# Row-maximum spread matmuls moved back in TensorE's order, and v's maxima taken one tile ahead

## The chip, the cores and the metric

The kernel runs on one core of a Trainium2 chip. The metric is the device time of one execution in microseconds (us). Five engines run beside each other, each taking its own instructions in order: TensorE (PE, the matmuls; PEld is its weight load), VectorE (DVE), ScalarE (ACT), GpSimd (POOL) and SyncE (SP, which here issues the transfers). They wait for each other through semaphores.

## The reference

Three parts follow one another on a batch of 4, 12 heads, 448 positions and 64 elements a head (768 in all):

```python
def _attn_ref(q, k, v):
    scores = scale * np.matmul(q, k.transpose(0, 1, 3, 2)) - np.log(S)
    attn = 1.0 / (1.0 + np.exp(-scores))
    return np.matmul(attn, v).astype(np.float32)

def _moe_ref(x, w_ch1, w_ch2):
    X = np.fft.fft(x, axis=1)
    X = np.fft.fft(X, axis=2)
    u = x + np.real(X)
    mu = np.mean(u, axis=-1, keepdims=True)
    var = np.mean((u - mu) ** 2, axis=-1, keepdims=True)
    un = (u - mu) / np.sqrt(var + 1e-06)
    ch = np.maximum(un @ w_ch1, 0.0) @ w_ch2
    return (u + ch).astype(np.float32)

def _moe2_ref(x, w_val, conv_w, w_out):
    for k in range(K):
        gate_pre += conv_w[k][None, None, :] * xp[:, k:k + S, :]
    gate = 1.0 / (1.0 + np.exp(-gate_pre))
    val = x @ w_val
    return (gate * val @ w_out).astype(np.float32)
```

## The kernel before

**Number formats.** The large products are made of f16 halves: a tensor is scaled by a power of two, rounded to f16 (`hi`, `hh`, `ph`, `xs` and so on), and what is left over is a second f16 tensor (`lo`, `hl`, `pl`). Each product takes three matmuls. The power of two comes from the largest absolute value of the tensor: v for each batch (it scales the Fourier mixing), w1 and w2 of the first weight group, and x2, the FFN's output, for each batch.

**The maximum and its spread.** `amax` (L104) reduces a tile to a column of row maxima. When all columns are there, `peak_row` (L107) reduces them to one column `t` and multiplies the identity `eye` by it, which gives the diagonal tile `pd` (L112, VectorE; one buffer). `peak_spread` (L115, the matmul at L118, TensorE) multiplies a matrix of ones by `pd`, so that each row of a PSUM tile holds all 128 maxima. `peak_max` (L121, the reduction at L123, VectorE) takes their maximum, and a chain of small operations makes the scale of it. The spread's tile is one of four `ps_m` buffers, which attention's output, the Fourier products, the norms, the down tiles and the value tiles share too. `peak` (L126) does the three as a generator: `wait` yields ahead of the spread, and as many behind it. Weights of later groups use `peak_pool`, which has no matmul.

**The order.** It is written by hand. The attention loop goes over 96 tiles, `t`, of two half heads; `b = t // 24` is the batch and `r = t % 24` the tile in it. In a tile TensorE gets the scores of tile t+1 (L356, L358) and, LAG tiles behind, the values (L381, L383); ScalarE the sigmoid (L369). `load_v` issues a v tile, `amax_v` takes its maximum, for four tiles at a time. `peak_v(b, k)` is step k of the three for v, and `scale_v` makes the scales. Three queues of generators are stepped within the loop: `fq` (Fourier mixing of the batch before), `lq` (norm) and `wq` (the conversion of 64-bit weights, `to_f32` and `split_weight`, on VectorE and ScalarE); `aq` is ScalarE's. VectorE's share in the loop is therefore the sum of maxima, folds (L399), weight conversion (L182 to L198), Fourier work (`eo`, `pl`, `zl`, L491, L494) and norm (L565 to L617).

**After the loop** the FFN runs as blocks of `up` (L730, ps_s) and `down` (L753, ps_m), weight group by weight group. Each yield of a block calls `background`, which steps the same queues; in the last group two steps of `wq` a call. ScalarE makes `hh` (L737), VectorE `hl` (L739) and adds down's product to `acc` (L757). As soon as `down` of the last group has finished batch b, `prep_x2(b)` is queued: six maxima (`xm`), the peak of them, the scale `sx`, then `xs` (ScalarE L795, VectorE L797). In the same stretch `first_gates` puts 24 convolution steps (L820) on VectorE. Then follow `value` (L907) and `project` (L932).

The steps of `peak` and the place of v's steps in the loop of the kernel before, in a few lines:

```python
    def peak(m, nm, wait):
        d = peak_row(m, nm)
        for _ in range(wait):
            yield
        p = peak_spread(d)
        for _ in range(wait):
            yield
        return peak_max(p, nm)
```

Of the kernel before, what the change touches and what calls it, by code (L numbers as in the profile page):

```python
# [17 lines left out]
B, H, S, D, DM, DFF = 4, 12, 448, 64, 768, 3072  # L18
CK = 112
NT = 6  # L20
# [41 lines left out]
def body(tc, qd, kd, vd, w1d, w2d, cwd, wvd, wod, cdd, k12d, csd, eyed, out):  # L62
# [60 lines left out]
        V.tensor_reduce(out=g, in_=p[:, :128], axis=AX.X, op=ALU.max)  # L123
        return g

    def peak(m, nm, wait):  # L126

        d = peak_row(m, nm)
        for _ in range(wait):
            yield  # L130
        p = peak_spread(d)
        for _ in range(wait):
            yield
        return peak_max(p, nm)

# [67 lines left out]
    def split_weight(pl, scratch, src, res, shape, exp, nm, bufs=1):  # L203

        n = shape[1] * shape[2]
        t = wp.tile([128, n], F32, tag="wf", bufs=1, name="wf")
        m = keep.tile([128, 18], F32, tag="wm", bufs=2, name="wm")
        step = scratch.cols
        yield from to_f32(scratch, src, t, n, m)
        yield  # L210
        m = m[:, :n // (step if step == WCOLS else step // 2)]
        g = yield from (peak(m, nm, 2) if step == WCOLS else peak_pool(m, nm))
        e, i = pow2(g, nm, True)
        s = scaled(i, 2.0 ** exp, nm + "s")
        yield
        scratch.idle = True
        while isinstance(pl, Later) and pl.at is None:
            yield
        scratch.idle = False
        step = scratch.cols  # L220
        hi = pl.tile(shape, F16, tag=nm + "hi", bufs=bufs, name=nm + "hi")
        lo = pl.tile(shape, F16, tag=nm + "lo", bufs=bufs, name=nm + "lo")
        res += [hi, lo, e]
        h, l = (x.rearrange("p a b -> p (a b)") for x in (hi, lo))
        for c in range(0, n, n // 4):
            cc = slice(c, c + n // 4)
            if step > WCOLS:
                A.activation(out=t[:, cc], in_=t[:, cc], func=AF.Copy, scale=s)
                A.activation(out=h[:, cc], in_=t[:, cc], func=AF.Copy)
                yield  # L230
                P.tensor_tensor(out=l[:, cc], in0=t[:, cc], in1=h[:, cc], op=ALU.subtract)  # L231
            else:
                yield from act(out=h[:, cc], in_=t[:, cc], func=AF.Copy, scale=s)
                V.scalar_tensor_tensor(out=l[:, cc], in0=t[:, cc], scalar=s, in1=h[:, cc], op0=ALU.mult, op1=ALU.subtract)
            yield
# [403 lines left out]
    for t in range(NHALF):  # L639
        i, g = t // 2, t % 2  # L640
        b = i // H
        r = t - b * 2 * H
        if t + 1 < NHALF:
            scores(t + 1)
        sigmoid(t)
        if t % 4 < 2 and t // 4 + 1 < NPAIR:
            (prep_k if t % 4 else prep_q)(t // 4 + 1)
        if t % 4 == 1 and t // 4 + 4 < NPAIR:
            load_qk(t // 4 + 4)
        if t % 4 == 1 and t // 4 + 2 < NPAIR:  # L650
            load_v(*divmod(t // 4 + 2, NT))
        if t % 4 == 2:
            amax_v(b, r // 4)
        if r == 23:
            peak_v(b, 0)
        if b and r == 0:
            peak_v(b - 1, 1)
        if b and r == 1:
            peak_v(b - 1, 2)
            scale_v(b - 1)  # L660
        if b and r == 2:
            fq.append(fourier(b - 1))
        step(fq)
        for n in range(3):
            if mixed.get(n) == 1:
                lq.append(norm(n))
            if n in mixed:
                mixed[n] += 1
        step(lq)
        if b == 0 and r in (6, 7, 8, 9):  # L670
            c, o = divmod(r - 6, 2)
            nc.sync.dma_start(out=cd[:, c, o], in_=cdd[:, c, o])
        if b == 0 and r == 12:
            nc.sync.dma_start(out=k12, in_=k12d)
        if b == 0 and r in (5, 6, 10, 11):
            c, o = divmod((5, 6, 10, 11).index(r), 2)
            cst.append(fk.tile([128, 3, 4 * NE], F32, tag="pm", bufs=2, name="cst")[:, :, :NP])
            nc.sync.dma_start(out=cst[-1], in_=csd[:, c, o])
        if b == 0 and r in (8, 9, 14, 15):
            c, o = divmod((8, 9, 14, 15).index(r), 2)  # L680
            push(out=cs[:, c, o], in_=cst.pop(0), func=AF.Copy)
        for n in range(2):
            if r == FOLD_AT + LAG + 4 * n:
                fold_part(b, n)
        if t > 6:
            credit[0] += W_RATE[0] if b == 0 else W_RATE[1] if r < 6 else W_RATE[2]
            step(wq, int(credit[0]))
            credit[0] %= 1
        drain(2 if t % 4 == 3 else 1)
        if t >= LAG:  # L690
            values(t - LAG)
            store_x(t - LAG)
    for t in range(NHALF - LAG, NHALF):
        values(t)
        store_x(t)
    peak_v(B - 1, 1)
    drain()
    finish(wq)
    peak_v(B - 1, 2)
    scale_v(B - 1)  # L700
    attn.close()


# [77 lines left out]
    def prep_x2(b):  # L781
        xs = acc[b][:, :, PAD:]
        m = keep.tile([128, NT], F32, tag="xm", bufs=2, name="xm")
        for j in range(NT):
            amax(xs[:, j], m, j)
            if j % 2:
                yield
        g = yield from peak(m, "x2", 1)
        e, i = pow2(g, "x2")
        sx = scaled(i, 2.0 ** X2_EXP, "sx")  # L790
        xs2 = homes[b].tile([128, NT, 2 * S], F16, tag=f"un{b}", name="xs")
# [249 lines left out]
```

## Time and profile before

| | us |
|---|---|
| time, median of 3 runs | 1113.61 (1111.94 to 1113.67) |
| the profiled execution | 1113.55 |
| its span, first to last instruction | 1111.8 |
| mean granted TensorE clock | 0.986 |
| TensorE busy | 1066.1 (96% of the span) |
| VectorE busy | 756.1 (68%) |
| ScalarE busy | 427.7 (38%) |
| GpSimd busy | 191.1 (17%) |

The span begins and ends with the first and the last instruction; the time of an execution holds a little more on both sides. Busy shares are means over stages that have different limits, so the rows below are read stage by stage. In a row of a timeline the first two numbers are start and duration in us, a group `x2` is two of the same form one behind the other, and the bracket at the end is the time that the engine stood idle ahead of it and what ended that. The granted clock is the share of full speed that TensorE was given.

### The profile page before, as it was taken

How to read it: one execution, taken by the hardware profiler on the slowest of the kernel's cores; microseconds unless marked ns; L12 is line 12 of the kernel's file. 1: busy time of each engine (PE TensorE's matmuls, PEld its weight loads, DVE VectorE, ACT ScalarE, POOL GpSimd, SP SyncE). 2: the span in 40 equal slices, each digit the busy share in tenths (PEclk: the TensorE clock that was granted, in tenths of full speed). 3: DMA queues.
4: the chain of work that ended last, by engine and by line, in shares of the span. 5: the costliest groups of instructions: out<-in, count | busy, mean ns of one | idle time of the engine just before them, and what ended most of it. 6: DMA issues, size and time to landing. Idle time of an engine off the chain costs nothing.

```text
span 1111.8 us, 15303 instructions
## 1 busy us (share of the span) xinstructions
PE 1066.1 (96%) x5616; PEld 550.7 (50%) x5616; DVE 756.1 (68%) x2154; ACT 427.7 (38%) x654; POOL 191.1 (17%) x171
## 2 busy tenths in 40 slices
PE   8899998989899999999999999999999967999998
PEld 4345453546455555555555555555555533555554
DVE  2866999697884676657676765676765679775530
ACT  5675656633232233333423233333233322343321
POOL 3322323331311111111101111110111100000000
PEclk9999999999999999999999999999999978999999
DMA  6723433011111322222333321233321100000001
GB/s 212 211 79 92 122 98 86 10 44 44 30 43 43 86 72 69 73 63 68 85 86 86 81 67 39 72 85 86 87 73 40 32 1 0 1 34 34 34 34 67
DMA packets 34780, 74.13 MB, mean 67 GB/s; under 512 B 3940, under 2 KB 11920, under 8 KB 34704
## 3 DMA queue, kind: packets, MB, share of 16 engines
q1 hardware_dynamic: 34704, 73.15, 23.2%
q8 instruction: 44, 0.72, 0.3%
q14 instruction: 32, 0.26, 0.1%
HBM read 67.46 MB, written 5.51 MB: 66 GB/s over the span
## 4 chain that ended last, share of the span: by engine, by line
PE 76%; DVE 16%; DMA 3%; ACT 3%; issue 1%; POOL 1%; SPq 0%; ACTq 0%; DVEq 0%; POOLq 0%
PE ps_s L730 26%; PE ps_m L753 26%; PE ps_m L932 7%; PE ps_m L907 7%; DMA w<-w1d 3%; PE ps_m L466 2%; PE ps_m L381 2%; PE ps_s L356 2%; PE ps_m L483 1%; DVE gp L820 1%; DVE wf L195 1%; DVE wf L198 1%; DVE xm L105 1%; DVE acc L757 1%; DVE wabs L190 1%
## 5 line engine op out<-in xcount | busy, mean ns | idle before, releaser
L730 PE MATMUL ps_s<-un,w1hi 128*128 128x448 f16 x1152 | 316.6, 357 | 3.5 <-DVE hl L739 3.5
L753 PE MATMUL ps_m<-hh,w2hi 128*128 128x448 f16 x576 | 205.1, 356 | 1.3 <-DVE acc L757 1.2
L730 PE MATMUL ps_s<-un,w1lo 128*128 128x448 f16 x576 | 205.5, 357 | 0.0
L753 PE MATMUL ps_m<-hl,w2hi 128*128 128x448 f16 x576 | 204.9, 356 | 0.0
L753 PE MATMUL ps_m<-hh,w2lo 128*128 128x448 f16 x576 | 204.7, 355 | 0.0
L730 PEld LDWEIGHTS <-w1hi 128*128 128x128 f16 x1152 | 113.5, 99 | 111.0 <-issue 8.8
L753 PEld LDWEIGHTS <-w2hi 128*128 128x128 f16 x1152 | 113.3, 99 | 108.5 <-issue 6.0
L757 DVE SCALAR_TENSOR_TENSOR acc<-ps_m,rg,acc 128x448 f32<-128x448 f32 x192 | 129.1, 678 | 41.8 <-PE ps_m L753 41.7
L179 ACT ACTIVATE wabs<-w 128x384 f32<-128x384 f32 (+1 forms) x109 | 58.4, 548 | 213.0 <-DMA w<-w2d 78.8
L739 DVE SCALAR_TENSOR_TENSOR hl<-ps_s,hh 128x896 f16<-128x896 f32 x64 | 54.6, 854 | 93.0 <-ACT hh L737 92.9
L190 DVE TENSOR_SCALAR_CACHE_REDUCE wabs<-wabs 128x192 f32<-128x192 f32 (+1 forms) x234 | 74.6, 353 | 35.9 <-ACT wabs L179 35.1
L369 ACT ACTIVATE sg<-ps_s,logb 128x896 f32<-128x896 f32 x96 | 86.3, 913 | 26.7 <-PE ps_s L356 22.4
L737 ACT ACTIVATE hh<-ps_s 128x896 f16<-128x896 f32 x64 | 46.2, 722 | 110.4 <-PE ps_s L730 110.4
L730 PEld LDWEIGHTS <-w1lo 128*128 128x128 f16 x576 | 56.9, 99 | 54.1 <-issue 2.5
L753 PEld LDWEIGHTS <-w2lo 128*128 128x128 f16 x576 | 56.8, 99 | 53.8 <-issue 2.0
L198 DVE SCALAR_TENSOR_TENSOR wf<-w,wf 128x192 int32<-128x192 int32 (+1 forms) x234 | 78.1, 371 | 0.3
L907 PE MATMUL ps_m<-xs,wvhi 128*128 128x448 f16 x288 | 78.0, 353 | 0.0
L195 DVE SCALAR_TENSOR_TENSOR wf<-w,wf 128x192 int32<-128x192 int32 (+1 forms) x234 | 77.0, 366 | 0.4
L192 DVE TENSOR_SCALAR wf<-wabs 128x192 int32<-128x192 int32 (+1 forms) x234 | 55.4, 275 | 31.7 <-POOL w1lo L231 12.7
L381 PE MATMUL ps_m<-sg,v 128*64 128x448 f32 x288 | 69.8, 564 | 0.0
L804 DVE SCALAR_TENSOR_TENSOR gp<-acc,cw,gp 128x448 f32<-128x448 f32 x72 | 49.3, 685 | 25.0 <-ACT gp L802 23.1
L932 PE MATMUL ps_m<-gh,wolo 128*128 128x448 f16 x144 | 50.8, 352 | 0.0
(187 smaller groups left out, 1398.4 us busy)
## 6 DMA issues: line engine op xcount, KB each, us to landing
w<-w1d SPq DMA_DIRECT2D x42, 384.0 KB
w<-w2d SPq DMA_DIRECT2D x42, 384.0 KB
k<-kd SPq DMA_DIRECT2D x24, 256.0 KB
v<-vd SPq DMA_DIRECT2D x24, 256.0 KB
q<-qd SPq DMA_DIRECT2D x24, 224.0 KB
out<-o SPq DMA_DIRECT2D x24, 224.0 KB
w<-wvd SPq DMA_DIRECT2D x12, 384.0 KB
w<-wod SPq DMA_DIRECT2D x12, 384.0 KB
```

The lines of the kernel that those rows point to most:

```text
L179: A.activation(out=wa, in_=z[:, :, 1].bitcast(F32), func=AF.Abs)
L190: V.tensor_scalar(out=a, in0=a, scalar1=LEAST, scalar2=None, op0=ALU.max, op1=ALU.max, accum_out=m[:, i:i + 1])
L192: V.tensor_scalar(out=f.bitcast(I32), in0=a.bitcast(I32), scalar1=0x07FFFFFF, scalar2=3, op0=ALU.bitwise_and, op1=ALU.logical_shift_left)
L195: V.scalar_tensor_tensor(out=f.bitcast(I32), in0=lo, scalar=29, in1=f.bitcast(I32), op0=ALU.logical_shift_right, op1=ALU.bitwise_or)
L198: V.scalar_tensor_tensor(out=f.bitcast(I32), in0=hi, scalar=-0x40000000, in1=f.bitcast(I32), op0=ALU.bitwise_and, op1=ALU.bitwise_or)
L369: A.activation(out=sg[:, :n], in_=sc.pop(t)[:, :n, :S], func=AF.Sigmoid, scale=1.0 / math.sqrt(D), bias=logb)
L381: nc.tensor.matmul(p[hs, :S], v[:, s, hs], a[:, h], start=(s == 0), stop=False)
L730: nc.tensor.matmul(p[:, i, :S], w[:, k, fs], u[:, k], start=(m == 0), stop=(m == 17))
L753: nc.tensor.matmul(p[:, :S], w[:, f, js], hh[f // 2][k][:, f % 2], start=(m == 0), stop=(m == 3 * FC - 1))
L757: V.scalar_tensor_tensor(out=acc[b][:, j, PAD:], in0=p[:, :S], scalar=rg, in1=acc[b][:, j, PAD:], op0=ALU.mult, op1=ALU.add)
L907: nc.tensor.matmul(p[:, :S], w[:, k, js], u[:, k], start=(n == 0), stop=(n == 17))
L932: nc.tensor.matmul(p[:, :S], w[:, k, js], gs[b, k][i], start=(n == 0), stop=(n == 17))
```

## The change

`peak` has two counts now: the yields ahead of the spread and those behind it. For w1 and w2 of the first group they go from 2 and 2 to 4 and 2, for x2 from 1 and 1 to 5 and 1. `amax_v` runs one v tile ahead: v tile 0 at t = 0, tile j+1 where tile j was taken. The six columns of a batch are therefore there four tiles sooner, and `peak_v`'s three steps stand at r = 19, 21 and 22 of the same batch, where they stood at r = 23 and at r = 0 and 1 of the next. For the last batch nothing is left behind the loop.

```diff
-    def peak(m, nm, wait):
+    def peak(m, nm, wait, after=1):
 
         d = peak_row(m, nm)
         for _ in range(wait):
             yield
         p = peak_spread(d)
-        for _ in range(wait):
+        for _ in range(after):
             yield
         return peak_max(p, nm)
...
-        g = yield from (peak(m, nm, 2) if step == WCOLS else peak_pool(m, nm))
+        g = yield from (peak(m, nm, 4, 2) if step == WCOLS else peak_pool(m, nm))
...
-        if t % 4 == 2:
-            amax_v(b, r // 4)
-        if r == 23:
+        if t == 0:
+            amax_v(0, 0)
+        if t % 4 == 2 and t // 4 + 1 < NPAIR:
+            amax_v(*divmod(t // 4 + 1, NT))
+        if r == 19:
             peak_v(b, 0)
-        if b and r == 0:
-            peak_v(b - 1, 1)
-        if b and r == 1:
-            peak_v(b - 1, 2)
-            scale_v(b - 1)
+        if r == 21:
+            peak_v(b, 1)
+        if r == 22:
+            peak_v(b, 2)
+            scale_v(b)
...
-    peak_v(B - 1, 1)
     drain()
     finish(wq)
-    peak_v(B - 1, 2)
-    scale_v(B - 1)
     attn.close()
...
-        g = yield from peak(m, "x2", 1)
+        g = yield from peak(m, "x2", 5)
```

Lines behind the loop have a number lower by one in the changed kernel (L730 is L729, L753 is L752, L757 is L756, L820 is L819).

TensorE's order at the first spread of v, at the end of batch 0, before:

```order
L356 MATMUL ps_s<-qh,kh 128x448 x2
L356 MATMUL ps_s<-qh,kl 128x448 x2
L356 MATMUL ps_s<-ql,kh 128x448 x2
L118 MATMUL ps_m<-pd,ones_r 128x128
L383 MATMUL ps_m<-sg,v 128x448
L356 MATMUL ps_s<-qh,kh 128x448 x2
```

and in the changed kernel, where it stands three tiles earlier:

```order
L356 MATMUL ps_s<-qh,kl 128x448 x2
L356 MATMUL ps_s<-ql,kh 128x448 x2
L118 MATMUL ps_m<-pd,ones_r 128x128
L381 MATMUL ps_m<-sg,v 64x448 x2
L358 MATMUL ps_s<-qh,kh 128x448
L358 MATMUL ps_s<-qh,kl 128x448
```

The spread is now taken between the scores and the values of another tile, and VectorE's row maximum and `pd` stand two weight chunks further forward than they did (behind L192 of chunk 7 of 9, no longer of chunk 9).

VectorE's order from the first `pd` of x2, in the FFN's tail (`acc_90` and `acc_92` are batches 0 and 1), before:

```order
L110 TENSOR_REDUCE x2t<-xm 128x1
L112 TENSOR_SCALAR pd<-eye,x2t 128x128
L123 TENSOR_REDUCE x2g<-ps_m 128x1
L152 TENSOR_SCALAR x2e<-x2g 128x1
L153 TENSOR_SCALAR x2e<-x2e 128x1
L155 RECIPROCAL x2i<-x2e 128x1
L160 TENSOR_SCALAR sx<-x2i 128x1
L797 SCALAR_TENSOR_TENSOR xs<-acc_90,sx,xs 128x3x448
L820 SCALAR_TENSOR_TENSOR gp<-acc_90,cw,gp 128x448 x2
L797 SCALAR_TENSOR_TENSOR xs<-acc_90,sx,xs 128x3x448
```

and in the changed kernel:

```order
L110 TENSOR_REDUCE x2t<-xm 128x1
L112 TENSOR_SCALAR pd<-eye,x2t 128x128
L819 SCALAR_TENSOR_TENSOR gp<-acc_90,cw,gp 128x448 x4
L738 SCALAR_TENSOR_TENSOR hl<-ps_s,hh 128x896
L123 TENSOR_REDUCE x2g<-ps_m 128x1
L152 TENSOR_SCALAR x2e<-x2g 128x1
L153 TENSOR_SCALAR x2e<-x2e 128x1
L155 RECIPROCAL x2i<-x2e 128x1
L160 TENSOR_SCALAR sx<-x2i 128x1
L796 SCALAR_TENSOR_TENSOR xs<-acc_90,sx,xs 128x3x448 x2
```

Four gate steps and an `hl` stand between `pd` and the reduction of the spread now, where nothing did.

TensorE's order at the second spread of x2, before, among up's matmuls:

```order
L730 LDWEIGHTS w1lo
L730 MATMUL ps_s<-un,w1lo 128x448
L118 MATMUL ps_m<-pd,ones_r 128x128
L730 LDWEIGHTS w1hi
L730 MATMUL ps_s<-un,w1hi 128x448
```

and in the changed kernel, 36 matmuls further back, among down's:

```order
L752 LDWEIGHTS w2lo
L752 MATMUL ps_m<-hh,w2lo 128x448
L118 MATMUL ps_m<-pd,ones_r 128x128
L752 LDWEIGHTS w2hi
L752 MATMUL ps_m<-hh,w2hi 128x448
```

The `up` block that stood behind the spread stands ahead of it.

## Rows read from the trace of the kernel before

**Rows 1.** Waits of TensorE by releaser: us in total, times, longest.

```profile
PE ps_m L118 <- DVE pd L112: 19.6, 7, 5.2
```

**Rows 2.** Busy time by stage: bounds, length, busy of each engine, clock, DMA share, GB/s.

```profile
0.00:231.40 231.40, 216.64 (x1169) 109.84 (x1170) 171.48 (x389) 146.56 (x212) 69.32 (x63) 1.00 0.36 109
231.40:247.40 16.00, 11.33 (x58) 5.51 (x57) 15.57 (x30) 3.59 (x6) 10.63 (x9) 0.93 0.17 53
...
311.00:889.00 578.00, 577.25 (x3052) 298.48 (x3051) 383.13 (x1375) 190.06 (x303) 94.64 (x87) 1.00 0.26 69
889.00:944.10 55.10, 39.71 (x167) 18.55 (x166) 46.61 (x83) 15.66 (x19) 0.00 (x0) 0.81 0.00 0
944.10:1111.80 167.70, 163.80 (x866) 84.43 (x863) 87.49 (x145) 51.84 (x86) 0.00 (x0) 1.00 0.09 34
```

**Rows 3.** Timeline of TensorE in the FFN's tail.

```profile
895.69 0.47 PE L118 MATMUL ps_m<-pd,ones_r 128*128 128x128 f32 x1 [4.82 <-DVE pd L112]
...
897.11 0.95 PE L730 MATMUL ps_s<-un,w1hi 128*128 128x448 f16 x2
...
910.05 0.47 PE L118 MATMUL ps_m<-pd,ones_r 128*128 128x128 f32 x1 [4.80 <-DVE pd L112]
...
935.89 0.47 PE L118 MATMUL ps_m<-pd,ones_r 128*128 128x128 f32 x1 [5.22 <-DVE pd L112]
```

**Rows 4.** Timeline of VectorE in the FFN's tail.

```profile
895.35 0.29 DVE L112 TENSOR_SCALAR pd<-eye,x2t 128x128 fp32r<-128x128 f32 x1
...
898.74 1.62 DVE L797 SCALAR_TENSOR_TENSOR xs<-acc,sx,xs 128x1344 f16<-128x1344 f32 x1 [1.48 <-ACT xs L795]
901.07 1.40 DVE L820 SCALAR_TENSOR_TENSOR gp<-acc,cw,gp 128x448 f32<-128x448 f32 x2 [0.71 <-ACT gp L817]
902.39 1.61 DVE L797 SCALAR_TENSOR_TENSOR xs<-acc,sx,xs 128x1344 f16<-128x1344 f32 x1
903.92 1.14 DVE L105 TENSOR_REDUCE xm<-acc 128x1 f32<-128x448 f32 x2
...
906.29 1.08 DVE L739 SCALAR_TENSOR_TENSOR hl<-ps_s,hh 128x896 f16<-128x896 f32 x1
...
922.56 0.68 DVE L757 SCALAR_TENSOR_TENSOR acc<-ps_m,rg,acc 128x448 f32<-128x448 f32 x1
```

**Rows 5.** Timeline of TensorE in attention, batch 0 and batch 2.

```profile
47.40 0.97 PE L381 MATMUL ps_m<-sg,v 128*64 128x448 f32 x4
...
55.13 0.33 PE L118 MATMUL ps_m<-pd,ones_r 128*128 128x128 f32 x1 [2.52 <-DVE pd L112]
...
172.94 0.33 PE L118 MATMUL ps_m<-pd,ones_r 128*128 128x128 f32 x1 [1.31 <-DVE pd L112]
```

**Rows 6.** Timeline of VectorE, end of batch 0.

```profile
46.32 0.65 DVE L192 TENSOR_SCALAR wf<-wabs 128x256 int32<-128x256 int32 x1
```

**Rows 7.** Timeline of VectorE, end of batch 1.

```profile
96.69 0.38 DVE L491 TENSOR_TENSOR sp<-sp,ps_m 6x226 f32<-6x226 f32 x1 [1.08 <-PE ps_m L483]
...
107.57 1.37 DVE L112 TENSOR_SCALAR pd<-eye,vt 128x128 fp32r<-128x128 f32 x1
```

**Rows 8.** Timeline of GpSimd at the same place.

```profile
107.58 1.28 POOL L310 TENSOR_TENSOR kl<-k,kh 128x512 fp32r<-128x512 f32 x1 [5.69 <-ACT kh L309]
```

**Rows 9.** Busy time in a stretch of batches 1 and 2, columns as in rows 2.

```profile
100.00:150.00 50.00, 47.84 (x257) 23.41 (x257) 47.91 (x112) 31.75 (x47) 16.28 (x12) 1.00 0.38 113
```

**Rows 10.** Timeline of TensorE at the Fourier products of batch 1.

```profile
131.20 0.70 PE L466 MATMUL ps_m<-cd,pl 128*113 128x385 f16 x3 [1.28 <-DVE pl L438]
```

**Rows 11.** Timeline of SyncE: transfers issued.

```profile
45.65 3.54 SPq L171 DMA_DIRECT2D w<-w1d  x2
...
145.26 0.38 SPq L323 DMA_DIRECT2D v<-vd  x1
```

**Rows 12.** Timeline of VectorE: readers of transferred tiles.

```profile
50.75 0.29 DVE L182 TENSOR_SCALAR wabs<-w 128x256 int32<-128x256 int32 x1 [1.93 <-DMA w<-w1d]
...
151.54 0.68 DVE L105 TENSOR_REDUCE vm<-v 128x1 f32<-128x512 f32 x1
```

## What was predicted

> **What bounds it now.** I read the list of waits first, then busy time by stage, then the rows around each spread. The profiled execution took 1113.55 us, which is 0.06 below the median of the three runs (1113.61), with a span of 1111.8; every sum below is made against 1113.55. The reader should see that TensorE's largest single wait is the one that this change touches: the spread matmul at L118 waits for the diagonal tile `pd` that VectorE writes at L112, 19.6 us in seven places [rows 1]. The stages differ [rows 2]. From 311 to 889 us TensorE is busy 577.25 of 578 us, so nothing can be won there, and its 3052 matmuls come at 0.189 us each. From 944.1 on it is busy 163.80 of 167.7. What is left is the attention stage (216.64 of 231.4), the short stage behind it, and the tail of the FFN, 889 to 944.1, where TensorE is busy 39.71 of 55.1 us at a granted clock of 0.81, and VectorE 46.61. Three of the seven waits lie in that tail: 4.82, 4.80 and 5.22 us. Those in attention are 2.52 and 1.31, and two short ones make up the rest (0.9).
>
> **The tail, the term that matters most.** The four x2 spreads move back by four steps of `background`, the reduction that follows stays one step behind. In TensorE's order the four spreads stand 18, 36, 18 and 36 matmuls later. Nothing is added: VectorE's operations up to the first `pd` are the same ones in the same order, so `pd` is ready when it was, at 895.64. TensorE came to the spread at 895.69 − 4.82 = 890.87; 18 × 0.189 = 3.4 us more work stands ahead of it now, so it comes at 894.3 and waits 1.4 us instead of 4.82 [rows 3]. That does not mean that 4 + 4 + 4 us are won, because behind each of the long waits VectorE is the engine that is late. So I count VectorE from 895.64 to the update (L757 before, L756 after) that frees the `ps_m` buffer for the first value tile, with the operations that stand there in the new order and the starts and durations of [rows 4]: ten pairs of gate steps at 1.32 (13.2), a large and a small `hl` (1.5), two chains from the reduction of the spread to the first `xs` at 2.55 each, their wait for ScalarE included (898.74 less 895.69, less the spread's own 0.5; 5.1), four `xs` at 1.53 (6.1), twelve maxima at 0.57 (6.8), ten updates of `acc` at 0.60 (6.0), two `pd` with their row maximum at 0.5 (1.0), and one wait of 0.7 for a gate's copy. That is 40.4 us: the buffer is free at 936.0. The first value tile began at 944.1, so 8.1 us is the most that the tail can give, however the spreads are placed.
>
> TensorE takes some of that back. Of the 40.4 us, 17.4 lie ahead of the second `pd`, which is then ready at 913.1. TensorE, with 54 matmuls between the first two spreads, is there at 895.97 + 54 × 0.189 = 906.2: a wait of about 7, longer than before, in place of the 4.80. The third `pd` has 36.0 of them ahead of it and is ready at 931.7; TensorE has 72 matmuls to it, 12 of them slow (below), and is there at 913.4 + 12 × 0.37 + 60 × 0.189 = 929.2, a wait of 2.5 in place of 5.22. Then the last down tile needs a buffer that VectorE frees a pair of gate steps and an update later (933.6), and its nine matmuls come after idle time, at the lower of the two clocks, 1.2 GHz (two take 0.95 us behind the 4.82 wait [rows 3], so 0.37 each, twice the 0.189; I count 12 of them behind a long wait): 933.6 + 3.4 = 937.0, and some three slow ones of the value tile make 937.6. The gain is 944.1 − 937.6 = 6.5; if the 1.4 us wait also drops the clock, the first pair of hidden tiles, and VectorE's chain behind it, are 1.3 late. I take **−6.0**, with −8.1 as the one end. The other end is −3.5: the second and third waits as long as before, the first shortened alone.
>
> In the tail VectorE, at 46.61 of 55.1 us [rows 2], is the fullest engine, and that is the ground for the second rival below. The Trainium skill, Perfetto Trace Analysis, section Identifying Performance Opportunities, says that the most-contended engine is the one of highest occupancy and is to be optimized first; by it a move of TensorE's waits that leaves VectorE its work would give nothing in the tail. The trace agrees in part: VectorE still has 8.5 us idle there, and 40.4 us of work up to the first value tile where it took 48.5.
>
> **Attention.** Batch 0: TensorE reaches the new place of v's spread, three half-head tiles earlier, at about 47.4; it stood at 55.13 and waited 2.52 [rows 5]. The new order puts v's row maximum and `pd` behind the L192 that starts at 46.32 [rows 6] and takes 0.65: ready at 47.4. The wait all but goes: −2.4. The short wait at w1's spread goes too, since that spread moves back behind more than a whole tile: −0.7. Batch 1 has no wait to remove, but the spread's work moves. Its `pd` took 1.37 us at 107.57, while GpSimd held a subtraction from 107.58 to 108.86 [rows 7, 8]; now it stands just ahead of the 96.69 operation, in front of which VectorE idles 1.08. From 100 to 150 us VectorE is busy 47.91 of 50 [rows 9], and TensorE waits 1.28 for it at the end [rows 10], so what leaves this stretch counts: between 0.4 (a bare `pd` and row maximum) and 1.5. I take −0.9.
> The Trainium skill, SBUF — State Buffer, section Who interferes with whom, has an exclusive lock on a port pair that VectorE and GpSimd share, under which the loser stands still for the other's whole instruction. The trace agrees here: `pd` 0.29 alone, 1.37 beside the subtraction. By the lock the gain is the whole 1.5, by the bare work 0.4.
> Batch 2's 1.31 also goes from the list, but VectorE is full around it, and I expect TensorE to wait for a sigmoid instead: 0. In sum **−4.0**, between −2 (only batch 0, partly) and −5.5 (batch 2's 1.31 too). The extra cost that I can find is one v maximum that runs a tile sooner, 0.68 us that is only moved.
>
> **Behind attention.** The last batch's reduction and scale now stand inside the loop and no longer behind the drain. VectorE is busy 15.57 of these 16 us [rows 2], so at most its 0.43 idle can go, and a worse order costs the same 0.4 or a few times that: −0.4, between −1.5 and +1.5. The remaining weights use the other form of reduction and are untouched.
>
> Sum: −6.0 − 4.0 − 0.4 = −10.4; 1113.55 − 10.4 = **1103.1 us**.
>
> **Rivals.**
> *Only the tail holds.* VectorE, full from 100 on, hands attention's gain back as later sigmoid and fold waits; for it the 47.91 of 50, against it the long idle stretches of VectorE ahead of 100, where batch 0's gain arises. 1113.55 − 6.0 = 1107.5.
> *Only attention holds.* VectorE's order decides the tail, the removed waits return at the second spread and at buffers; for it 46.61 of 55.1, against it the 40.4 counted. 1113.55 − 4.4 = 1109.2. The Trainium skill's rule on the most-contended engine (Perfetto Trace Analysis, Identifying Performance Opportunities) would give this time.
> *Slower: VectorE waits for v.* The maxima now run a tile ahead. VectorE takes its instructions in order, so a maximum whose v has not landed holds all weight conversion, and with it `zl`, `pl` and the sigmoids' partners. The narrowest place in the full stretch: the v tile issued at 145.26 is now read where the tile before it was read, near 151.54, 6.3 us later [rows 11, 12]. A transfer of the same 256 KB took 5.1, from 45.65 to its first reader at 50.75, which waited 1.93 for it. It decides from landings of about 8 us on: the eight or so tiles of that stretch then give the gain back. At 10 us and four tiles as narrow as this one, 4 × 3.7 = 14.8 comes back: 1117.9.
> *No effect.* All waits only change their name: 1113.5.
>
> **Chances.** My forecast 0.66; only the tail 0.12; only attention 0.12; no effect 0.06; slower 0.04. The range for eight in ten takes in both half cases and the far end of the bounds (−8.1 − 5.5 − 1.5 = −15.1): 1098.5 to 1110. Within 0.2%, 2.2 us, is about what a measurement of this kernel can't tell from no change. The last two cases and the slow edge of the half cases give faster 0.86, same 0.08, slower 0.06.
>
> **What the new profile should show.** L118's total falls from 19.6 to about 11, with one long wait of about 7 at the second x2 spread, 1.4 at the first and 2.5 at the third, and none over 0.5 in attention's batches 0 and 1. The first FFN matmul comes 4 us sooner, the first value tile 10 sooner, near 934; the stretch of pure FFN and the end after the first value tile keep their lengths within 1 us. I am wrong if VectorE shows waits for v's transfer, if the second wait in the tail grows past 9, if value tiles wait for gates, or if TensorE's waits for sigmoids grow by what L118 loses.

## The result, and the profile after

The changed kernel took 1103.12 us (median of four runs, 1102.64 to 1104.18) beside 1113.64 for the kernel before: a ratio of 0.9914 (0.9897 to 0.9931). The forecast was 1103.1. The profiled execution has a span of 1101.6 us where it was 1111.8. That a sum comes out right says little about its terms, so each is read by itself.

TensorE's waits, by what released them (us in total, times, longest). The changed kernel's list:

```profile
PE ps_m L118 <- DVE pd L112: 11.5, 4, 7.0
PE ps_s L356 <- ACT sg L369: 5.3, 6, 2.6
...
PE ps_m L752 <- DVE acc L756: 1.6, 1, 1.6
...
PE ps_m L906 <- DVE gp L911: 0.7, 1, 0.7
```

L118 fell from 19.6 us in seven places [rows 1] to 11.5 in four. Down's wait for a buffer (L752) stood in the list before too, 1.2 us in three places; the value tile's wait for a gate product (the last line) is new.

Busy time by stage in the changed kernel; the bounds follow the stages of [rows 2] (columns as there):

```profile
0.00:227.10 227.10, 218.29 (x1169) 110.74 (x1170) 172.05 (x396) 146.66 (x212) 70.03 (x63) 0.99 0.36 111
227.10:243.10 16.00, 11.84 (x60) 5.92 (x59) 14.72 (x24) 4.87 (x8) 10.51 (x9) 0.96 0.27 77
307.00:884.10 577.10, 577.10 (x3053) 298.49 (x3052) 381.15 (x1373) 189.16 (x302) 95.41 (x87) 1.00 0.26 69
884.10:932.60 48.50, 36.43 (x167) 17.67 (x166) 43.50 (x81) 12.28 (x17) 0.00 (x0) 0.85 0.00 1
932.60:1101.60 169.00, 164.78 (x866) 84.71 (x863) 90.66 (x146) 54.75 (x89) 0.00 (x0) 0.99 0.09 33
```

Three stages changed. Attention ends 4.3 us sooner, the tail is 6.6 shorter, and the value and output stage is 1.4 longer. TensorE had 231.4 − 216.64 = 14.8 us without a matmul in attention and has 8.8 now; in the tail it had 15.4 and has 12.1, and the granted clock is 0.85 in place of 0.81.

TensorE in the tail of the changed kernel, at the first three x2 spreads and behind the third:

```profile
890.75 0.33 PE L118 MATMUL ps_m<-pd,ones_r 128*128 128x128 f32 x1 [1.41 <-DVE pd L112]
...
908.31 0.47 PE L118 MATMUL ps_m<-pd,ones_r 128*128 128x128 f32 x1 [7.00 <-DVE pd L112]
...
927.21 0.33 PE L118 MATMUL ps_m<-pd,ones_r 128*128 128x128 f32 x1 [2.08 <-DVE pd L112]
929.12 0.53 PE L752 MATMUL ps_m<-hh,w2hi 128*128 128x448 f16 x1 [1.58 <-DVE acc L756]
...
932.43 0.95 PE L906 MATMUL ps_m<-xs,wvhi 128*128 128x448 f16 x2
```

And VectorE there, at the three `pd` and at the updates that free TensorE's buffers:

```profile
890.41 0.29 DVE L112 TENSOR_SCALAR pd<-eye,x2t 128x128 fp32r<-128x128 f32 x1
...
907.97 0.29 DVE L112 TENSOR_SCALAR pd<-eye,x2t 128x128 fp32r<-128x128 f32 x1
...
926.87 0.29 DVE L112 TENSOR_SCALAR pd<-eye,x2t 128x128 fp32r<-128x128 f32 x1
927.07 1.40 DVE L819 SCALAR_TENSOR_TENSOR gp<-acc,cw,gp 128x448 f32<-128x448 f32 x2
928.39 0.68 DVE L756 SCALAR_TENSOR_TENSOR acc<-ps_m,rg,acc 128x448 f32<-128x448 f32 x1
...
930.30 1.27 DVE L756 SCALAR_TENSOR_TENSOR acc<-ps_m,rg,acc 128x448 f32<-128x448 f32 x2
```

The last block's up begins 4.94 us sooner in this execution (884.07 for 889.01), so 4.94 is to be added before these starts are set beside the ones forecast. The reader should see that the waits are the ones counted (1.4, 7, 2.5 and a buffer 2 us behind the third `pd`), that one of them is longer than any was before, and that the gain is there nevertheless: what sets the first value tile is VectorE's row at 928.39, and not the sum of TensorE's waits. That update ends at 929.07, and the last down tile, which needs its buffer, begins at 929.12. It is nine matmuls at 0.37 us each, and the first value tile follows them at 932.43 without a wait. Its own buffer, freed by the first of the two updates from 930.30, had been there since 930.9. From 929.0 to 934.7 the granted clock was 0.51; at 0.189 us each the nine would have taken 1.7 us and not 3.3.

In attention, TensorE at v's spread of batch 0, at the Fourier products of batch 1, and at a tile of batch 3:

```profile
46.85 0.33 PE L118 MATMUL ps_m<-pd,ones_r 128*128 128x128 f32 x1 [1.03 <-DVE pd L112]
...
126.25 0.70 PE L466 MATMUL ps_m<-cd,pl 128*113 128x385 f16 x3 [0.90 <-DVE pl L438]
...
183.28 0.47 PE L356 MATMUL ps_s<-qh,kh 64*128 64x448 f32 x2 [2.60 <-ACT sg L369]
```

Batch 0's wait is 1.03 and not gone; batch 2's 1.31 has gone, and the wait for a sigmoid soon behind it, 1.85 before, is 2.60. Behind that wait the granted clock is 0.62 from 183.0 to 187.5 us, where it was 1.00 before.

VectorE at a v maximum near the start and at batch 1's `pd`, and GpSimd beside the latter:

```profile
14.60 0.69 DVE L105 TENSOR_REDUCE vm<-v 128x1 f32<-128x512 f32 x1 [3.08 <-DMA v<-vd]
...
91.73 0.29 DVE L112 TENSOR_SCALAR pd<-eye,vt 128x128 fp32r<-128x128 f32 x1
...
90.59 1.28 POOL L310 TENSOR_TENSOR kl<-k,kh 128x512 fp32r<-128x512 f32 x1 [4.61 <-ACT kh L309]
```

The first is the wait of the slower rival: it exists, and nothing follows from it, since VectorE's next work waits for w1's transfer until 25.00. The second is the 1.37 us of [rows 7], now 0.29 at a place where GpSimd is ending such a subtraction (90.59 to 91.87) and no longer beginning one.

### The profile page after: what moved, and what is told of

It reads as the page before. It is cut to its first block, busy times and chain, and to the rows that moved or that the text cites. A ratio compares the mean times of both kernels' runs of the same rounds, so it can differ in the third digit from the quotient of the medians.

```text
span 1101.6 us, 15310 instructions
## 1 busy us (share of the span) xinstructions
PE 1064.5 (97%) x5616; PEld 551.3 (50%) x5616; DVE 751.3 (68%) x2154; ACT 427.4 (39%) x654; POOL 192.9 (18%) x171
## 4 chain that ended last, share of the span: by engine, by line
PE 76%; DVE 18%; ACT 3%; DMA 1%; issue 1%; SPq 0%; POOL 0%; DVEq 0%; POOLq 0%; ACTq 0%
PE ps_m L752 27%; PE ps_s L729 27%; PE ps_m L931 7%; PE ps_m L906 6%; PE ps_s L356 2%; PE ps_m L466 2%; PE ps_m L381 2%; PE ps_m L483 1%; DVE gp L819 1%; DVE gp L803 1%; DMA w<-w1d 1%; DVE wf L198 1%; DVE xm L105 1%; DVE pm L399 1%; DVE wabs L190 1%
## 5 line engine op out<-in xcount | busy, mean ns | idle before, releaser
L729 PE MATMUL ps_s<-un,w1hi 128*128 128x448 f16 x1152 | 312.8, 353 | 4.2 <-DVE hl L738 4.2
L752 PE MATMUL ps_m<-hh,w2hi 128*128 128x448 f16 x576 | 205.1, 356 | 1.6 <-DVE acc L756 1.6
L752 PE MATMUL ps_m<-hl,w2hi 128*128 128x448 f16 x576 | 205.1, 356 | 0.0
L752 PE MATMUL ps_m<-hh,w2lo 128*128 128x448 f16 x576 | 204.9, 356 | 0.0
L729 PE MATMUL ps_s<-un,w1lo 128*128 128x448 f16 x576 | 203.5, 353 | 0.0
L729 PEld LDWEIGHTS <-w1hi 128*128 128x128 f16 x1152 | 112.8, 98 | 109.7 <-issue 6.3
L752 PEld LDWEIGHTS <-w2hi 128*128 128x128 f16 x1152 | 113.2, 99 | 107.8 <-issue 4.7
L756 DVE SCALAR_TENSOR_TENSOR acc<-ps_m,rg,acc 128x448 f32<-128x448 f32 x192 | 129.5, 679 | 45.1 <-PE ps_m L752 44.8
L752 PEld LDWEIGHTS <-w2lo 128*128 128x128 f16 x576 | 56.8, 99 | 53.7 <-issue 2.0
L729 PEld LDWEIGHTS <-w1lo 128*128 128x128 f16 x576 | 56.5, 98 | 52.9 <-issue 0.4
L906 PE MATMUL ps_m<-xs,wvhi 128*128 128x448 f16 x288 | 78.9, 356 | 0.7 <-DVE gp L911 0.7
L192 DVE TENSOR_SCALAR wf<-wabs 128x192 int32<-128x192 int32 (+1 forms) x234 | 53.8, 269 | 28.7 <-POOL w1lo L231 12.1
L906 PE MATMUL ps_m<-xs,wvlo 128*128 128x448 f16 x144 | 51.2, 355 | 0.0
```

The source lines that it names most:

```text
L729: nc.tensor.matmul(p[:, i, :S], w[:, k, fs], u[:, k], start=(m == 0), stop=(m == 17))
L752: nc.tensor.matmul(p[:, :S], w[:, f, js], hh[f // 2][k][:, f % 2], start=(m == 0), stop=(m == 3 * FC - 1))
L756: V.scalar_tensor_tensor(out=acc[b][:, j, PAD:], in0=p[:, :S], scalar=rg, in1=acc[b][:, j, PAD:], op0=ALU.mult, op1=ALU.add)
L906: nc.tensor.matmul(p[:, :S], w[:, k, js], u[:, k], start=(n == 0), stop=(n == 17))
```

## The experiments

The runs were made beside the kernel before, 4 to 12 executions of each, in four sets. In these sets the kernel before has medians of 1112.94 to 1113.64, and its single executions lie between 1109.7 and 1116.8; a ratio is taken within a set, so it says more than a difference between times of two sets. "Attention" is the start of the first matmul of up. "Tail" is the time from the first matmul of the last up block to the first value matmul in the profiled execution, "rest" from there to the end; the starts are those of the rows.

| run | time, us | ratio (95% interval) | attention, us | tail, us | rest, us |
|---|---|---|---|---|---|
| before | 1113.6 | 1 | 231.3 | 54.9 | 167.8 |
| changed | 1103.1 | 0.9914 (0.9897 to 0.9931) | 227.0 | 48.4 | 169.2 |
| x2 alone | 1107.65 | 0.9945 (0.9924 to 0.9966) | 232.3 | 47.9 | 168.7 |
| v alone | 1108.46 | 0.9958 (0.9943 to 0.9973) | 226.0 | 53.7 | 168.4 |
| w alone | 1112.32 | 0.9984 (0.9971 to 0.9998) | 228.8 | 55.0 | 167.8 |
| half the gate steps | 1097.6 | 0.9856 (0.9833 to 0.9878) | 227.9 | 40.9 | 169.4 |
| v's maxima ahead, alone | 1112.8 | 0.9997 (0.9984 to 1.001) | 231.1 | 55.2 | 167.8 |
| wait filled with matmuls | 1102.94 | 0.9899 (0.9886 to 0.9912) | 228.9 | 47.7 | 168.9 |
| nine yields | 1100.34 | 0.9877 (0.9861 to 0.9894) | 228.2 | 40.8 | 173.3 |
| gates on GpSimd | 1100.52 | 0.9877 (0.9864 to 0.989) | 225.0 | 42.8 | 172.5 |
| nine, and gates on GpSimd | 1096.63 | 0.9855 (0.9837 to 0.9872) | 228.1 | 38.0 | 171.6 |
| the same, later gates | 1094.03 | 0.9832 (0.9817 to 0.9846) | 227.1 | 38.0 | 168.8 |
| nine, later gates | 1097.44 | 0.9862 (0.9846 to 0.9878) | 226.4 | 40.8 | 170.1 |

**The x2 spreads alone.**

```diff
-        g = yield from peak(m, "x2", 1)
+        g = yield from peak(m, "x2", 5)   # on the kernel before, w1 and w2 kept at 2 and 2
```

> The kernel before with the x2 spreads alone moved (5 yields ahead, 1 behind); v's maxima, v's spreads and those of w1 and w2 stand as they were. My account of the tail gives -6.0 us against the kernel before: about 1107.6, with TensorE waits of about 1.4, 7 and 2.5 us at the first three x2 spreads in place of 4.82, 4.80 and 5.22. The rival, that VectorE's order decides the tail whatever TensorE waits for, gives 1113 to 1114, the first value tile no sooner than 55 us behind the 889 mark. A third reading, that the profiled runs differ mostly by chance in attention and the tail holds the whole gain, gives about 1103.

Measured 1107.65, −5.3 by the medians of the same rounds. TensorE in the tail of this run:

```profile
896.07 0.33 PE L118 MATMUL ps_m<-pd,ones_r 128*128 128x128 f32 x1 [1.41 <-DVE pd L112]
...
913.63 0.47 PE L118 MATMUL ps_m<-pd,ones_r 128*128 128x128 f32 x1 [7.00 <-DVE pd L112]
...
932.30 0.33 PE L118 MATMUL ps_m<-pd,ones_r 128*128 128x128 f32 x1 [2.40 <-DVE pd L112]
934.21 0.53 PE L753 MATMUL ps_m<-hh,w2hi 128*128 128x448 f16 x1 [1.58 <-DVE acc L757]
```

The four waits of the account stand there with nothing else changed. The rival that the tail gives nothing is out, and so is the third reading, that it gave all of the 10 us.

**v alone.**

```diff
-        g = yield from (peak(m, nm, 4, 2) if step == WCOLS else peak_pool(m, nm))
+        g = yield from (peak(m, nm, 2, 2) if step == WCOLS else peak_pool(m, nm))
-        g = yield from peak(m, "x2", 5)
+        g = yield from peak(m, "x2", 1)   # on the changed kernel
```

> The changed kernel with w1's, w2's and x2's spreads put back (2 and 2, 1 and 1): only v's maxima a tile ahead and v's three steps within their own batch. The account gives -3.7 for v (2.4 at batch 0's spread, 0.9 in the full stretch of batch 1, 0.4 behind the loop): about 1109.9. If the gain of 1.4 us that the changed kernel's profile shows between 20 and 28 us, far from any spread, is chance in the landing of transfers, it is -2 to -2.5: about 1111.3. The rival that VectorE, full from 100 us on, gives attention's gain back, gives 1113 to 1114.

Measured 1108.46, −4.5 (the interval reaches from −3.0 to −6.3). The gain is there, nearer the whole sum than the cut one; that VectorE hands it back is out. At batch 0's spread TensorE waits for nothing in this run:

```profile
45.92 0.33 PE L118 MATMUL ps_m<-pd,ones_r 128*128 128x128 f32 x1
```

**w1's and w2's spreads alone.**

```diff
-        g = yield from (peak(m, nm, 2) if step == WCOLS else peak_pool(m, nm))
+        g = yield from (peak(m, nm, 4, 2) if step == WCOLS else peak_pool(m, nm))   # on the kernel before
```

> The kernel before with w1's and w2's spreads alone moved (4 yields ahead instead of 2). The account gives -0.7, the wait at w1's spread: about 1112.9, which five rounds hardly tell from 1113.6; the profile should show no wait at w1's spread (0.68 before), and attention's end sooner by 0.7 or not at all. If w conversion is what TensorE really waits for, two more yields make it later and the time is 1114 or more.

Measured 1112.32, −0.6 (by the ratio −1.8, between −0.2 and −3.2), and no wait at w1's spread is left in its profile. By the medians the three parts give −5.3 − 4.5 − 0.6 = −10.4, and the whole change gave −10.5. By the ratios they give −6.1 − 4.7 − 1.8 = −12.6, and the whole −9.6 (between −7.7 and −11.5). So the parts add within their intervals, some 3 us; that they add to 0.1 is luck.

**Half the gate steps left out.** This kernel's gate of batch 0 is another one, since two of the four later taps aren't added.

```diff
             for k in range(1, 5):
-                V.scalar_tensor_tensor(out=gp, in0=acc[0][:, j, k:k + S], ...)
+                if k % 2:
+                    V.scalar_tensor_tensor(out=gp, in0=acc[0][:, j, k:k + S], ...)
```

> The changed kernel with 12 of the 24 gate steps of batch 0 left out on VectorE in the tail (taps 2 and 4 of the convolution are not added, so the gate is another one); all yields, and so TensorE's order, stay. If VectorE's work decides when the first value tile can start, as my count of 40.4 us says, the 10 pairs in that count become 10 single steps and the first value tile comes up to 6.6 us sooner; TensorE's wait at the second x2 spread falls from 7.0 to about 4 and the time to 1097 to 1098.5. If TensorE's own order and clock decide the tail, the waits shrink by under 1 us and the time stays within 1 us of 1103.1.

Measured 1097.6, −5.5 against the changed kernel's 1103.1. TensorE's order is untouched. Its waits in the tail, and its first value tile (L907 here), are now:

```profile
905.68 0.48 PE L118 MATMUL ps_m<-pd,ones_r 128*128 128x128 f32 x1 [5.08 <-DVE pd L112]
...
922.77 0.33 PE L118 MATMUL ps_m<-pd,ones_r 128*128 128x128 f32 x1 [1.69 <-DVE pd L112]
923.96 0.35 PE L752 MATMUL ps_m<-hh,w2hi 128*128 128x448 f16 x1 [0.86 <-DVE acc L756]
...
925.66 0.54 PE L907 MATMUL ps_m<-xs,wvhi 128*128 128x448 f16 x2
```

The tail is 7.5 us shorter. The buffer of the last down tile is free 5.9 us sooner, counted from the start of the last up block (39.15 for 45.05 us), so VectorE's work decides when that tile begins. The other 1.6 us are TensorE's: the nine matmuls behind it now run at the full clock and take 1.70 us in place of 3.31. The expectation's 6.6 had put all of it on VectorE.

**v's maxima ahead, alone.**

```diff
-        if t % 4 == 2:
-            amax_v(b, r // 4)
+        if t == 0:
+            amax_v(0, 0)
+        if t % 4 == 2 and t // 4 + 1 < NPAIR:
+            amax_v(*divmod(t // 4 + 1, NT))   # on the kernel before
```

> The kernel before with v's maxima taken a tile ahead and nothing else: v's row maximum, spread and reduction stand where they stood. If v's gain comes from the place of the spread, nothing is won here: 1112.5 to 1113.5, with the wait at batch 0's spread (2.52 before) still there, and the cost of reading v a tile sooner is seen by itself, as waits of VectorE for v's transfer (one of 3.1 us in the changed kernel, at 14.6) that no other engine passes on. If the gain came with the maxima, by other landings of transfers, the time is near that of the v part alone, 1108.5 to 1110. If waiting for v costs anything, it is over 1114.

Measured 1112.8, ratio 0.9997: the maxima by themselves win and cost nothing that shows (between −1.8 and +1.1 us). One point of the expectation failed. TensorE did not wait at batch 0's spread in this profile, and attention is as long as before all the same. TensorE's rows are these:

```profile
38.08 0.74 PE L356 MATMUL ps_s<-qh,kh 64*128 64x448 f32 x2 [2.89 <-ACT sg L369]
...
55.43 0.33 PE L118 MATMUL ps_m<-pd,ones_r 128*128 128x128 f32 x1
```

and ScalarE's row just ahead of the first of them:

```profile
36.98 0.52 ACT L260 ACTIVATE cs<-cst 128x384 fp32r<-128x384 f32 x1 [4.03 <-DMA cst<-csd]
```

ScalarE stood 4.03 us for a table's transfer (2.96 in the kernel before), and TensorE waited 2.89 us for the sigmoid behind it (1.81 before). Then TensorE's clock was low, where the kernel before had 1.00 from 36 to 46 us:

```profile
38.00:44.30 6.30, 6.22 (x18) 2.46 (x18) 5.84 (x17) 4.78 (x8) 2.00 (x2) 0.51 0.53 153
```

So TensorE came to the spread late, and `pd`, begun at 54.87 (54.79 before), was ready. The spread's wait is what is left after such delays.

**The second wait filled.** 28 matmuls of ones by ones go into the spread's own buffer ahead of the second x2 spread; their result is overwritten.

```diff
         p = ps_m()
+        for _ in range(fill):
+            nc.tensor.matmul(p[:, :128], ones, ones, start=True, stop=True)
         nc.tensor.matmul(p[:, :128], ones_r, d, start=True, stop=True)
...
-        g = yield from peak(m, "x2", 5)
+        g = yield from peak(m, "x2", 5, 1, 28 if b == 1 else 0)
```

> The changed kernel with 28 matmuls of ones by ones (128 columns, results overwritten) ahead of the second x2 spread, so that TensorE works through most of its 7.0 us wait there and its clock has no reason to fall. If VectorE decides the tail, as counted, the matmuls behind the spread run at the full clock but the third pd comes when it came: its wait grows from 2.4 to about 4.5, the first value tile moves by under 0.8 us, and the time stays at 1102.5 to 1103.5. If the lower clock behind the long wait is what costs, the 2.2 us of slow matmuls come back in full: 1101.

Measured 1102.94. Behind the filled wait the granted clock is full. Busy time there, in this run and below it in the changed kernel (columns as in [rows 2]):

```profile
909.90:914.60 4.70, 4.66 (x25) 2.53 (x26) 4.59 (x9) 0.17 (x1) 0.00 (x0) 1.00 0.00 0
```

```profile
908.00:914.20 6.20, 5.89 (x17) 2.59 (x18) 5.50 (x13) 0.75 (x2) 0.00 (x0) 0.50 0.00 0
```

TensorE's waits in the tail of this run (lines higher by two) are:

```profile
909.94 0.33 PE L120 MATMUL ps_m<-pd,ones_r 128*128 128x128 f32 x1 [0.73 <-DVE pd L112]
...
922.44 0.35 PE L754 MATMUL ps_m<-hh,w2hi 128*128 128x448 f16 x1 [1.57 <-DVE acc L758]
...
928.61 0.33 PE L120 MATMUL ps_m<-pd,ones_r 128*128 128x128 f32 x1 [2.40 <-DVE pd L112]
930.52 0.35 PE L754 MATMUL ps_m<-hh,w2hi 128*128 128x448 f16 x1 [1.58 <-DVE acc L758]
```

In the changed kernel fifteen matmuls behind the spread took 5.59 us, 2.8 more than at 0.189 each. What the clock gives back there returns for the most part as a new wait of 1.57 for a buffer; at the third spread, where the expectation had put it, the wait is 2.40 for 2.08. The time has not moved beyond its interval, and the tail is 0.6 us shorter. So behind the second spread the lower clock costs little, because VectorE is later still. That doesn't hold for the nine matmuls behind the last buffer, which this run left slow in the main (2.95 us): two runs with less work on VectorE, half the gate steps and the gates on GpSimd, have them at the full clock, and the first value tile the sooner for it.

**Nine yields.**

```diff
-        g = yield from peak(m, "x2", 5)
+        g = yield from peak(m, "x2", 9)
```

> The changed kernel with 9 yields ahead of the x2 spreads in place of 5. By the account of VectorE the row maximum and the diagonal of batch 2 and its four long maxima (3 us in all) move behind the update that frees the first value tile's buffer, while everything else in the count stays: the first value tile comes 2 to 3 us sooner and the time is 1100.5 to 1101.5. If what counts is TensorE's waits at the spreads, which were already short at the first, it is within 1 us of 1103.1; if the later scale of x2 holds the value tiles of batches 1 to 3, it is slower, 1104 to 1106, with waits of TensorE at L906.

Measured 1100.34. The tail lost 7.5 us, more than the 2 to 3 expected, and the rest gained 4.1. Its rows of VectorE, at the update that frees the first value tile's buffer, and of TensorE, at the first value tile and at the first output tile:

```profile
925.22 0.68 DVE L756 SCALAR_TENSOR_TENSOR acc<-ps_m,rg,acc 128x448 f32<-128x448 f32 x1
...
925.96 0.73 PE L906 MATMUL ps_m<-xs,wvhi 128*128 128x448 f16 x2 [2.11 <-DVE acc L756]
...
959.38 0.35 PE L931 MATMUL ps_m<-gh,wohi 128*128 128x448 f16 x1 [1.42 <-ACT gh L914]
```

The long waits at the spreads are gone. Laid beside the changed kernel's, VectorE's rows show the 7.5. Behind the first `pd`, the work up to the update that counts is 4.2 us shorter: a `pd` with its row maximum, six maxima and one `xs` of later batches now stand behind it (some 5.2 us together), and two waits for ScalarE, 0.9 in sum, are new. The other 3.3 us are the nine slow matmuls, which no longer lie between that update and the first value tile, because it now frees that tile's own buffer.

The 4.1 us given back are 2.8 of waits and 1.3 of matmuls at the lower clock. The longest wait, 1.42, is that of the first output tile for the last `gh` of batch 0, a second place where VectorE's work comes late.

**Gates on GpSimd.** For the last two of six feature tiles of batch 0, ScalarE multiplies and GpSimd adds.

```diff
+                if j in (4, 5):
+                    s = keep.tile([128, S], F32, tag="gsc", bufs=3, name="gsc")
+                    A.activation(out=s, in_=acc[0][:, j, k:k + S], func=AF.Copy, scale=cw[:, j, k:k + 1])
+                    P.tensor_tensor(out=gp, in0=gp, in1=s, op=ALU.add)
+                else:
                     V.scalar_tensor_tensor(out=gp, in0=acc[0][:, j, k:k + S], ...)
```

> The changed kernel with the gates of two of the six feature tiles of batch 0 (the last two) taken from VectorE: ScalarE multiplies each tap, GpSimd, idle in this stage, adds it. Eight gate steps, 5.3 us, leave VectorE's count of 40.4, two pairs of them ahead of the third pd and two behind it. If VectorE decides the tail, the wait at the third spread (2.4) goes and the first value tile comes 3.5 to 5 us sooner: 1098.5 to 1100. If TensorE's order decides, the time stays within 1 us of 1103.1. If GpSimd's additions slow VectorE's operations beside them, or hold ScalarE's queue and with it xs of batch 2, half of it or more is lost: 1101 to 1103.

Measured 1100.52, between two of the readings. The tail is 5.6 us shorter, and 3.3 of it is given back behind it. Of the 5.6, 4.0 are VectorE's: three of the four pairs removed stood ahead of the update that frees the last down tile's buffer. The other 1.6 are the nine matmuls behind it, at the full clock again. TensorE's rows (L911 and L936 are L906 and L931 of the changed kernel):

```profile
906.41 0.47 PE L118 MATMUL ps_m<-pd,ones_r 128*128 128x128 f32 x1 [6.99 <-DVE pd L112]
...
923.26 0.35 PE L752 MATMUL ps_m<-hh,w2hi 128*128 128x448 f16 x1 [0.18 <-DVE acc L756]
...
924.96 0.54 PE L911 MATMUL ps_m<-xs,wvhi 128*128 128x448 f16 x2
...
958.20 0.35 PE L936 MATMUL ps_m<-gh,wohi 128*128 128x448 f16 x1 [2.25 <-ACT gh L919]
```

The second spread's wait is untouched (the steps removed stand behind it), the third's is gone, and the wait for `gh` is there as with nine yields.

**Both, and the gates behind moved by a tile.** The first run has nine yields and the gates on GpSimd. The second has the later gates too, which are one number:

```diff
-        i = t + 2
+        i = t + 1
```

The third has nine yields and the later gates, without GpSimd. The three expectations, in this order:

> The kernel with 9 yields and the gates of two feature tiles on ScalarE and GpSimd, together. If VectorE's work up to the first value tile were the only bound, the two gains add: 1103.1 - 2.8 - 2.6 = 1097.7 or less, since both runs gave some 3 us of their earlier first value tile back (TensorE waited 1.4 and 2.2 us for gh at the first output tiles). If that later bound, VectorE's work up to the last gh of batch 0, has taken over, the nine-yield run's gain is used up there and only the removed 5.3 us of gate steps count behind it: 1097 to 1098, with the wait at the first output tile grown to 4 or 5 us. If ScalarE's longer queue holds xs or gh, it is 1099 to 1101.

> As the one before, with the gates of batches 1 to 3 issued one tile later (the tile after next's gate becomes the next one's), so that one group of four gate steps (2.85 us) no longer stands ahead of the last two gl of batch 0. If VectorE's work up to the last gh of batch 0 is the second bound, TensorE's wait at the first output tile shrinks by 2 to 3 us and the time is 1094.5 to 1096. If it is not, it stays with the one before, 1097 to 1098; if a value tile then waits for its gate, it is slower than that by 1 or more.

> The changed kernel with 9 yields ahead of the x2 spreads and the gates of batches 1 to 3 one tile later, nothing on GpSimd. The nine-yield run took 1100.3 and waited 1.4 us for gh and 1.1 for a gate product in the value stage. If these waits come from gate steps standing ahead of gl, they go: 1098 to 1099. If VectorE is simply full there, the waits return a few tiles later: 1100 to 1101.

Both together took 1096.63, within the first reading, still with a wait of 1.43 us for `gh` at the first output tile, not the 4 or 5 of the second:

```profile
955.49 0.35 PE L936 MATMUL ps_m<-gh,wohi 128*128 128x448 f16 x1 [1.43 <-ACT gh L919]
```

With the later gates that wait is no longer in the trace, and the time is 1094.03, ratio 0.9832 (0.9817 to 0.9846), a little below the range expected. Without GpSimd, nine yields and later gates took 1097.44, 0.6 under the range; the wait for `gh` is gone there too. Busy time in the tail of the fastest:

```profile
885.40:923.50 38.10, 31.77 (x166) 16.09 (x165) 32.68 (x58) 15.86 (x23) 5.18 (x5) 1.00 0.00 1
```

VectorE's work in the tail is 32.7 us in place of 43.5, TensorE keeps the full clock through it, and the rest takes 168.8 us again, 1.0 more than before the change.

## Why the prediction was right

**The tail.** Forecast −6.0, with waits of 1.4, 7 and 2.5 and a late buffer; the profile has 1.41, 7.00, 2.08 and 1.58, and x2 alone took 5.3 us off. Set in the old frame, the `pd`s were forecast at 895.64, 913.1 and 931.7 and came, end of the row and 4.94, at 895.64, 913.2 and 932.1; the buffer at 936.0 came near 935.8 (the first of two updates from 930.30). It is not the one that decided, which the forecast had said too: the last down tile's buffer, forecast at 933.6, came at 934.0, the nine slow matmuls took 3.31 us where 3.4 were counted, and the first value tile, forecast at 937.6, came at 937.4. So the mechanism was the right one: VectorE's count up to that buffer, then nine slow matmuls, and not TensorE's waits. What the runs add is that this count can be shortened: the tail lost 7.5 us by leaving out gate steps, 5.6 by GpSimd and 7.5 by putting a batch's maxima behind the freeing update. In the first two 1.6 of these are the nine matmuls at the full clock; in the third 3.3 are the same nine, no longer in the way.

**What was mis-sized in it.** Behind the first value tile 1.4 us were given back, where the account had 0.55, three slow matmuls of that tile. Its first six matmuls took 2.23 us, 1.1 more than at 0.189 each, and a later value tile, at 971.91, waited 0.7 for a gate product. That is the row L906 in the list of waits; the nine-yield run has it too, 1.06 us at 968.45, beside its wait for `gh`. The prediction had kept the end after the first value tile within 1 us, and had named value tiles that wait for gates, and waits for v's transfer, as signs of being wrong. Both signs came, at a cost of 0.7 us and of nothing.

**Attention.** Forecast −4.0, −0.4 behind it. The profile gives −4.3 at the end of attention and −0.6 from there to the last block; v and w alone give −4.5 and −0.6. Batch 0's wait should have gone but for 0.1, and was 1.03 in this profile. TensorE came at 45.82, 1.6 us sooner than the 47.4 forecast, and `pd` was done at 46.79, only 0.6 sooner. The wait is not a constant. Where v's spread stands as before, the four profiles have 2.52 (before), 3.84 (x2 alone), 1.66 (w alone) and none (v's maxima ahead, alone), 2.0 on the mean; where it is moved, seven of nine have none, one 1.03 and one 1.04, 0.2 on the mean. So the term was read from one draw and is 1.8 rather than 2.4.

The profile's other 1.4 us in batch 0 come from elsewhere: near 22 us ScalarE waited 2.18 for a table's transfer in the kernel before and 0.88 in the changed one, and the sigmoids behind it start 1.4 us sooner. In x2 alone and w alone, which don't differ from the kernel before up to there, that wait is 1.07 and 0.84, so it is chance, not the change. Most of it went again in the 1.03 at the spread, where TensorE would not have waited had it come 1.4 us later; luck's share in the −4.3 is therefore about 0.4, an estimate from these two numbers.

Batch 1's 0.9 is borne out: `pd` took 0.29 us, TensorE's wait at the Fourier product fell from 1.28 to 0.90, and the sigmoids of v alone stand 1.2 us better behind that stretch than ahead of it. That GpSimd's subtraction beside it was what made 1.37 of it is the reading of the Trainium skill (SBUF — State Buffer, Who interferes with whom); the traces agree: in the kernel before, x2 alone, w alone and v's maxima ahead this `pd` begins beside a subtraction and takes 1.37 or 1.38 us, in the changed kernel w2's `pd` at 170.08 took 1.11 us and ended 0.08 after the subtraction beside it, and every `pd` with GpSimd idle took 0.28 or 0.29. No run tried the pair alone.

Batch 2 is near its forecast: 1.31 gone at the spread, and the sigmoid's wait longer, 2.60 for 1.85, with the lower clock behind it.

**The rivals.** *Only attention* and *only the tail* are out by the runs of the parts: the intervals of x2 alone and of v alone both lie clear of no change. The Trainium skill's rule on the most-contended engine (Perfetto Trace Analysis, Identifying Performance Opportunities), which would have had the tail unchanged, does not hold as a bound here: VectorE was at 85% of the tail, 46.61 of 55.1 us, and moving TensorE's spreads took 6.6 us off it, as they also moved what VectorE does ahead of the freeing update. As advice on what is next it holds, since every later gain came from taking work from VectorE or from reordering it. *VectorE waits for v* did happen, 3.08 us once, with no one behind it; by itself the change of the maxima gave 0.9997. *No effect* is out.

**What stays open.** That the nine matmuls' clock is worth 1.6 us is read from runs that changed VectorE's work as well; no run changed their clock alone. Why v's `pd` of batch 0 is ready sooner in some profiles than in others (begun at 52.16 with w alone, at 54.68 to 54.87 in the other three that leave it in its place) was not followed up.

## What to carry to other kernels

When one engine waits for another's small operation, ask first what that other engine still has to do before the next thing that the first one needs, and sum it in its own order: moving the wait wins no more than that sum leaves, and a longer wait can be part of a gain. Then look for the next place of the same kind at once (here the last `gh` of batch 0), since an earlier start runs into it. And take a wait that hangs on a transfer from more than one run before it is put into a sum. A lower clock behind a wait is free only where the other engine is later still: here it cost little behind the second spread and, by the runs with less work on VectorE, 1.6 us in the last nine matmuls of down.

## What was not expected of the hardware

ScalarE's wait for the transfer of a small table near 22 us was 2.18, 1.07 and 0.84 us in three kernels that are the same up to there, and TensorE's wait at batch 0's spread, left in its place, went from none to 3.84 us. The traces show how the two can be tied. With x2 alone TensorE came to the spread 1.4 us sooner than in the kernel before (51.18 for 52.61), as ScalarE had waited less, but `pd` was begun when it always was (54.68 for 54.79), so the short wait for the table came back as a long one at the spread. With v's maxima ahead a longer wait for another table, and 6.3 us at half the clock behind it, left no wait at the spread. In the run with gates on GpSimd its addition of 448 f32 columns took 1.3 to 1.5 us each beside VectorE's work (5.38 and 5.98 us for four), twice VectorE's 0.66 for a multiply and an add; it still paid, in a stage where GpSimd had no other work.
